# First batch's token mix in the AV banks, beta as masked rows made on chip, and mixing out of the score banks

## The chip, the cores and the metric

The kernel runs on one core of a Trainium2 chip. The metric is the device time of one launch in microseconds (us), as the median of several executions. TensorE (PE) does the matmuls, VectorE (DVE) and ScalarE (ACT) the elementwise work, GpSimd (POOL) casts, copies and issues of converting loads, SyncE (SP) issues of plain loads, stores and DMA transposes.

## The reference

Eight batches of grouped-query attention (16 query heads on 4 key/value heads, 384 positions, head width 64) feed a residual MLP with affine steps over 1024 channels and 4096 hidden channels:

```python
attn = softmax(q @ k.T / sqrt(64)); x = (attn @ v) with heads side by side   # 384 x 1024
a1  = alpha1 * x + beta1
tok = einsum('ts,bsd->btd', w_tok, a1)
u   = x + lam * tok
a2  = alpha2 * u + beta2
out = u + lam * (relu(a2 @ w_ch1) @ w_ch2)
```

## The kernel before

**Stages.** `side(b)` returns a list of small units of work for batch b: transposes of k and q, scores, exp, AV, the token mix and the transposes of a2. `main(b)` is the channel MLP of batch b: 32 h matmul groups (L393, eight matmuls of 128x384 each) and then six output groups (L417, 32 matmuls of 128x512 each). Batch 0's units run alone at the start; batch b+1's units are slipped between the matmuls of `main(b)` at a steady pace. The order of each engine's instructions is the order of the program: `manual_schedule` reorders nothing, and each engine runs its queue in that order.

**Pairs.** Attention works on pairs of heads: `NP` = 8 pairs, each 128 channels. `scores(i)` (L202) fills 1024 score columns and ACT takes their exp (L211). `av_piece(p, hh)` (L236) gives one pair's AV; VectorE divides by the sum (`rinv` L241, `x` L242) and forms a1 (L246 in batch 0, L249 and L251 later). `tok(p)` (L258) mixes the pair over positions; VectorE adds it to x (L265) and forms a2 (L270). `a2_transpose(p)` turns a2 for the h matmuls, either as a DMA transpose issued by SyncE (L274) or on PE with an ACT copy (L280, L283).

**PSUM.** The eight banks are four tags: "sc" has two buffers of two banks (scores, and batch 0's first h groups), "mm" two of one bank (h, output groups, warm-up, and batch 0's AV), "av" and "tp" one bank each. A tile with the tag of another waits until that one has been read. Before the change `tok` takes "av" in batch 0 and "sc" later; `spread` (vectors) takes "tp" or "av".

**Batch 0's vectors.** alpha1*lam, alpha2, beta1*lam and lam are loaded as 24 rows (three copies of eight rows of 128) into `rows_f`, and `split` (L496 to L503) parts each into three bf16 rows that add up to the float32 value. `spread` multiplies them with a selector `sel`, which broadcasts a row over the 128 partitions, and ACT copies the result into `vecs` (L312). beta1 enters batch 0's mix another way: `rows_r` (L298 to L302) makes row sums of the transposed w_tok in two bf16 parts, `R`, and `H` holds beta in rows; one matmul of R by H for each third of the output adds the term (L262). H is filled by three small DMAs at the end of the second `split` (L505).

**Order in batch 0.** The dictionary `at` says which steps follow which `scores(i)`. Three pairs of q are transposed early, `spread` of the lower pairs follows scores 2 and 4, w_tok's transposes (`wtok_transpose`, L289 and L292) follow scores 4 and 5. At the end of `side(0)` the list of `a2_transpose`, `tok(6)`, `tok(7)` and `h_part` (the first four h groups, L147, cut by the eight pairs of channels they read) overlaps the mix of the last pairs with the first h matmuls. Pairs 0 to 3 of a2 go by DMA transpose, pairs 4 to 7 by PE.

**Weights.** w_ch1 comes in 16 chunks a batch through a ring of five buffers, by GpSimd's queue (L126); chunk c+5 is issued once chunk c has been used. w_ch2 is loaded once, in slices between batch 0's chunks (L131), and the next batch's q and v follow in the same queue (L108, L102).

Of the kernel before, what the change touches and what calls it, by code (L numbers as in the profile page):

```python
# [12 lines left out]
def kernel(  # L13
# [21 lines left out]
    nc = tc.nc  # L35
    f32 = mybir.dt.float32
# [11 lines left out]
    P = 128  # L48
# [86 lines left out]

    late = []


    early = {}

# [12 lines left out]
    def side(b):  # L153
# [11 lines left out]

        def bc(t, p):
            return t[:, None, cols(p)].to_broadcast([P, NST, P])

        def evac(eng):
            return nc.scalar.copy if eng == "ACT" else nc.vector.tensor_copy  # L170

        def k_transpose(h0, eng="DVE"):
            k2 = k2s[b]
# [77 lines left out]
            nc.vector.tensor_tensor(out=a1s[p], in0=t, in1=bc(h1, p), op=ADD)  # L251

        def tok(p):
            ps = psum.tile([P, NST, P], f32, tag="av" if first else "sc", name="tok",
                           bufs=1 if first else 2)
            for tt in range(NST):
                for st in range(NST):
                    nc.tensor.matmul(out=ps[:, tt, :], lhsT=wtokT[:, st, tt * P:(tt + 1) * P],  # L258
                                     rhs=a1s[p][:, st, :], start=(st == 0),
                                     stop=(st == NST - 1 and not first))  # L260
                if first:
                    nc.tensor.matmul(out=ps[:, tt, :], lhsT=R[:, tt * P:(tt + 1) * P],  # L262
                                     rhs=H[:, cols(p)], start=False, stop=True)
            u = x[:, :, cols(p)]
            nc.vector.tensor_tensor(out=u, in0=ps, in1=u, op=ADD)  # L265
            if first:
                a2s[p] = hTf[:, 7296 + p % 5 * S:7296 + (p % 5 + 1) * S].rearrange("p (a d) -> p a d", a=NST)
            else:
                a2s[p] = sb.tile([P, NST, P], bf, tag="a2", name="a2", bufs=3)
            nc.vector.tensor_tensor(out=a2s[p], in0=u, in1=bc(al2, p), op=MUL)  # L270

        def a2_transpose(p):
            if not pe_flip or first and p < NP - 4:
                nc.sync.dma_start_transpose(  # L274
                    out=a2T[:, p, :S].rearrange("p (a s) -> p a s", a=NST),
                    in_=a2s[p].rearrange("p a d -> p (a d)"))
                return
            ps = tp_ps([P, NST, P])
            for tt in range(NST):
                nc.tensor.matmul(out=ps[:, tt, :], lhsT=a2s[p][:, tt, :], rhs=ident,  # L280
                                 is_transpose=True, start=(tt == 0), stop=(tt == NST - 1),
                                 skip_group_check=True)
            nc.scalar.copy(out=a2T[:, p, :S], in_=ps.rearrange("p a b -> p (a b)"))  # L283
# [8 lines left out]
            nc.vector.tensor_copy(out=wtokT[:, st, :], in_=ps.rearrange("p a b -> p (a b)"))  # L292


        def rows_r(tag):
            ps = psum.tile([P, S], f32, tag=tag, name="r", bufs=1)
            for st in range(NST):
                nc.tensor.matmul(out=ps[:3], lhsT=ones3, rhs=wtokT[:, st, :], start=(st == 0),  # L298
                                 stop=(st == NST - 1))
            t = hTf[:3, 10240:10240 + S]  # L300
            nc.vector.tensor_copy(out=t, in_=ps[:3])
            nc.vector.scalar_tensor_tensor(out=R[:3], in0=t, scalar=neg3, in1=ps[:3], op0=MUL, op1=ADD)  # L302


        def spread(ps_, vs, tag, eng="ACT"):
# [18 lines left out]
        if not first:  # L324
            if pe_flip:
                add(k_transpose, 0)
                add(q_transpose, 0)
                add(k_transpose, 2)
                add(q_transpose, 2)
                if b == 1:  # L330
                    add(split, 3, 4)
            for j in range(NP + 4):
                if 1 < j < NP + 2:
                    add(av_piece, j - 2, 0)
                    add(av_piece, j - 2, 1)
                if j <= NP:
                    add(scores2, j)
                    if pe_flip and j in (1, 3):
                        add(q_transpose, 4 + 2 * (j // 2))
                if 2 < j < NP + 3:  # L340
                    add(tok if pe_flip else tok_flip, j - 3)
                if pe_flip and j > 3:
                    add(a2_transpose, j - 4)
                if b == 1 and j < 2:
                    for p in (4 * j, 4 * j + 2):
                        add(spread, (p, p + 1), (2, 4), "tp")
                elif j < 2:
                    us.extend([lambda: None] * 2)
            return us
# [1 line left out]
        add(q_transpose, 0, 1, "DVE", "av")  # L351
        add(q_transpose, 1, 1, "DVE", "tp")
        lower, upper = range(NP // 2), range(NP // 2, NP)
        at = {1: [(warmup, 3), (split, 0, 1), (split, 1, 3)], 2: [(warmup, 2), (spread, lower, (0, 1), "tp"), (warmup, 2)],
              3: [(q_transpose, 2, 2, "DVE", "av")],
              4: [(spread, lower, (1, 2), "tp"), (wtok_transpose, 0, "av"), (wtok_transpose, 1, "tp")],
              5: [(wtok_transpose, 2, "av"), (rows_r, "tp")],
              7: [(q_transpose, 4, 2, "ACT")], 8: [(k_transpose, 2, "ACT"), (spread, upper, (0, 1), "av")],
              10: [(q_transpose, 6, 2, "ACT")], 12: [(spread, upper, (1, 2), "tp")]}
        for i in range(18):  # L360
            add(scores, i)
            for f, *a in at.get(i, []):
                add(f, *a)
            for p in range(NP):
                last = (9 * p + 8) // 4
                if i == last + 1:
                    add(av_piece, p, 0)
                    add(av_piece, p, 1)
                if i == last + 4:
                    add(tok_flip if p < NP - 4 else tok, p)  # L370
        add(av_piece, NP - 1, 0)
        add(av_piece, NP - 1, 1)
        for f, *a in ((a2_transpose, 4), (tok, 6), (a2_transpose, 5), (h_part, (0, 1), range(4)), (tok, 7),
                      (a2_transpose, 6), (h_part, (2, 3), range(4)), (h_part, range(4), (4, 5)),
                      (a2_transpose, 7), (h_part, range(4), (6,)), (h_part, range(4), (7,))):
            add(f, *a)
        return us

# [51 lines left out]
    with tc.manual_schedule(engines=order):  # L430
# [9 lines left out]
        load_k(0, [0])  # L440

        hTf = hT.rearrange("p n s -> p (n s)")
        rows_f = hTf[:24, 9216:10240].bitcast(f32)
        rows_t = hTf[:24, 10240:11264].bitcast(f32)
        rows_b = hTf[:, 11264:11776]
        stage = sb.tile([P, NST * DM], f32, tag="x", name="stage", bufs=2)
        qst, vst = (stage[:, i:i + Hkv * NST * D].rearrange("p (h st d) -> p h st d", h=Hkv, st=NST)
# [2 lines left out]
        be2 = stage[:, 2112:2112 + NDT]  # L450
        R = stage[:, 2120:2312].bitcast(bf)
        H = stage[:, 2312:2824].bitcast(bf)
        ones3 = stage[:, 2824:2826].bitcast(bf)[:, :3]
        neg3 = stage[:3, 2826:2827]
        masks = [stage[:24, 2827 + i:2828 + i] for i in range(2)]
        sel = stage[:, 2829:2833].bitcast(bf)
        for t in (stage[:, 2120:2824], rows_b, sel):
            nc.vector.memset(t, 0.0)
        nc.sync.dma_start(out=vst, in_=v[0].rearrange("h (p st) d -> p h st d", st=NST))

        for i, ap in enumerate((moe_alpha1, moe_alpha2, moe_beta1, moe_lam)):
            nc.sync.dma_start(out=rows_f[:, i * P:(i + 1) * P],
                              in_=bass.AP(tensor=ap.tensor, offset=ap.offset, ap=[[0, 3], [P, NP], [1, P]]))
        load_k(0, [2])
        with nc.allow_non_contiguous_dma(reason="one small vector, once"):
            nc.sync.dma_start(out=be2, in_=moe_beta2.rearrange("(dt di) -> di dt", di=P))
# [11 lines left out]

        load_q4(1)
        make_identity(nc, ident)  # L480
        nc.gpsimd.memset(ones3, 1.0)
        nc.gpsimd.tensor_scalar(out=neg3, in0=ident[:3, 1:2], scalar1=-1.0, scalar2=None, op0=MUL)
        for t in vt:
            nc.vector.memset(t[:, :, :, D:], 1.0)
        AX = mybir.AxisListType.X
        for i, m in enumerate(masks):
            nc.vector.tensor_reduce(out=m, in_=ident[:24, 8 * (i + 1):24], op=ADD, axis=AX)
        with nc.allow_low_precision("ones and zeros"):
            nc.vector.tensor_reduce(out=sel[:24], in_=ident[:24, :24].rearrange("p (k c) -> p c k", k=3), op=ADD, axis=AX)

        def split(lo, hi):
            c = slice(lo * P, hi * P)
            for i in (0, 2):
                if lo <= i < hi:
                    r = rows_f[:, i * P:(i + 1) * P]
                    nc.vector.tensor_tensor(out=r, in0=r, in1=rows_f[:, 3 * P:], op=MUL)  # L496
            src, dst = rows_f, rows_t
            for m in masks:
                nc.vector.tensor_copy(out=rows_b[:24, c], in_=src[:, c])
                nc.vector.scalar_tensor_tensor(out=dst[:, c], in0=rows_b[:24, c], scalar=m, in1=src[:, c],  # L500
                                               op0=MUL, op1=mybir.AluOpType.subtract)
                src, dst = dst, src
            nc.vector.tensor_copy(out=rows_b[:24, c], in_=src[:, c])  # L503
            for i, k in enumerate((0, 0, 1)) if lo <= 2 < hi else ():
                nc.sync.dma_start(out=H[i:i + 1], in_=rows_b[8 * k:8 * k + 8, 2 * P:3 * P])  # L505

        place_k(0, 0)
        for h, cp in ((0, nc.vector.tensor_copy), (2, nc.scalar.copy)):
# [81 lines left out]
```

## Time and profile before

| | |
|---|---|
| median of 9 runs | 823.04 us (821.86 to 824.46) |
| profiled execution | 824.29 us |
| its span | 822.2 us, mean granted clock 0.993 |
| batch 0's units alone | first 50 us of the span |
| software DMA queue | 83.28 MB, 87.8% of 16 engines' span |

The page gives busy time by engine, and the span in 40 slices of 20.6 us each. A wait is named by the waiting engine, its tile and line, and what came last. The granted clock is PE's, as a share of full speed. Matmul ends are modelled, so a PE that is shown busy may still wait a little; start-to-start times of groups are safer than their lengths.

### The profile page before, as it was taken

Reading aid. Unit: us, or ns where it says so; the run is one execution under the profiler, and the core shown is the slowest. Engines: PE = TensorE matmul, PEld = TensorE weight load, DVE = VectorE, ACT = ScalarE, POOL = GpSimd, SP = SyncE. Lnnn points to the kernel's source line nnn. Section 1 sums busy time; section 2 is a strip of 40 time slices with the busy share of each in tenths; the row PEclk is TensorE's granted clock in tenths of the full one; section 3 lists DMA queues with packets and bytes.
Section 4 is the critical chain, followed back from the end, with each engine's and each line's share of the span. In section 5 each row is a group of like instructions: output and inputs, shape, how many; then the busy total and the mean of one; then the engine's idle time right before and its main releaser. Section 6 shows DMA issues by size and latency. Waiting matters only on the chain.

```text
span 822.2 us, 14049 instructions
## 1 busy us (share of the span) xinstructions
PE 802.1 (98%) x6072; PEld 448.3 (55%) x6072; DVE 346.4 (42%) x678; ACT 225.7 (27%) x299; POOL 185.3 (23%) x231
## 2 busy tenths in 40 slices
PE   6789999999999999999999999999999999999997
PEld 3655555565555655566545664556545565556543
DVE  6744545244543444434443344524454344442222
ACT  5725321332103421133212331033210442102100
POOL 6224440124002240022401233022500221003000
PEclk9999999999999999999999999999999999999999
DMA  9999999799949993599927999489994999129610
GB/s 165 199 161 200 201 214 177 122 177 171 93 102 160 177 159 59 130 172 174 146 63 137 180 176 109 98 134 178 174 85 98 147 178 127 36 57 192 87 39 38
DMA packets 261017, 112.94 MB, mean 137 GB/s; under 512 B 110204, under 2 KB 254684, under 8 KB 260956
## 3 DMA queue, kind: packets, MB, share of 16 engines
q0 software_dynamic: 197760, 83.28, 87.8%
q1 hardware_dynamic: 62652, 28.38, 14.2%
q8 instruction: 47, 0.77, 0.4%
q10 hardware_dynamic: 544, 0.39, 0.2%
q14 instruction: 14, 0.11, 0.0%
HBM read 170.51 MB, written 12.58 MB: 223 GB/s over the span
## 4 chain that ended last, share of the span: by engine, by line
PE 88%; DVE 2%; issue 0%; ACT 0%; ACTq 0%; DVEq 0%
PE ch L417 41%; PE h L393 36%; PE av L236 4%; PE sc L202 3%; PE tok L258 3%; DVE a1f L249 1%; DVE x L242 1%; DVE a L251 1%; DVE hT L403 0%; ACT es L211 0%; DVE rinv L241 0%; PE tp L280 0%; DVE o L422 0%; DVE o L423 0%; PE tp L186 0%
## 5 line engine op out<-in xcount | busy, mean ns | idle before, releaser
L417 PE MATMUL ch<-w,hT 128*128 128x512 bf16 x1536 | 353.5, 379 | 0.0
L393 PE MATMUL h<-a2T,w 128*128 128x384 bf16 (+1 forms) x2016 | 349.3, 326 | 0.6
L393 PEld LDWEIGHTS <-w 128*128 128x128 bf16 x2016 | 189.5, 98 | 124.8 <-issue 8.4
L126 POOL DMA_DIRECT2D w<-in_moe_w_ch_dram x128 | 112.6, 880 | 549.4 <-PE h L393 493.5
L417 PEld LDWEIGHTS <-hT 128*128 128x128 bf16 x1536 | 142.5, 98 | 155.2 <-issue 4.6
L211 ACT ACTIVATE es<-sc 128x1024 bf16<-128x1024 f32 x126 | 123.3, 1021 | 281.6 <-PE sc L202 281.6
L403 DVE TENSOR_SCALAR hT<-h,bias 128x384 bf16<-128x384 f32 x128 | 79.0, 617 | 187.1 <-PE h L393 186.5
L401 ACT ACTIVATE hT<-h,bias 128x384 bf16<-128x384 f32 x128 | 74.3, 581 | 227.2 <-PE h L393 202.4
L422 DVE TENSOR_TENSOR o<-ch,vecs 128x512 f32<-128x512 f32 x48 | 33.0, 688 | 92.6 <-PE ch L417 92.5
L265 DVE TENSOR_TENSOR x<-tok,x 128x384 f32<-128x384 f32 x64 | 35.5, 555 | 85.7 <-PE tok L258 77.1
L236 PEld LDWEIGHTS <-es 128*128 128x128 bf16 x1008 | 45.9, 97 | 21.4 <-ACT es L211 0.9
L236 PE MATMUL av<-v,es 128*128 128x65 bf16 x1008 | 49.2, 193 | 0.8 <-ACT es L211 0.8
L258 PEld LDWEIGHTS <-wtokT 128*128 128x128 bf16 x576 | 38.5, 99 | 15.6 <-issue 4.2
L202 PE MATMUL sc<-qT,kT 64*128 64x384 bf16 (+2 forms) x576 | 45.9, 275 | 0.3 <-ACT hT L211 0.3
L241 DVE RECIPROCAL rinv<-av 128x6 f32<-128x6 f32 x64 | 12.3, 192 | 67.6 <-PE av L236 67.3
L258 PE MATMUL tok<-a,wtokT 128*128 128x128 bf16 x504 | 37.3, 219 | 0.9 <-ACT es L211 0.9
L242 DVE TENSOR_TENSOR x<-av,rinv 128x384 f32<-128x384 f32 x64 | 35.6, 557 | 2.3
L202 PEld LDWEIGHTS <-kT 64*128 64x128 bf16 x576 | 20.0, 94 | 27.8 <-issue 23.3
L423 DVE TENSOR_TENSOR o<-o,x 128x512 f32<-128x512 f32 x48 | 33.3, 693 | 1.6
L270 DVE TENSOR_TENSOR a<-x,vecs 128x384 bf16<-128x384 f32 x56 | 31.5, 562 | 1.9
L251 DVE TENSOR_TENSOR a<-a1f,vecs 128x384 bf16<-128x384 f32 x56 | 31.2, 557 | 2.2
L249 DVE TENSOR_TENSOR a1f<-x,vecs 128x384 f32<-128x384 f32 x56 | 31.2, 557 | 1.9
(68 smaller groups left out, 211.6 us busy)
## 6 DMA issues: line engine op xcount, KB each, us to landing
w<-in_moe_w_ch_dram POOLq DMA_DIRECT2D x135, 512.0 KB, 6.5
out_dram<-o SPq DMA_DIRECT2D x48, 256.0 KB, 2.1
q_raw<-in_q_dram POOLq DMA_DIRECT2D x21, 256.0 KB, 7.8
kst<-in_k_dram SPq DMA_DIRECT2D x16, 192.0 KB, 3.0
w<-in_moe_w_ch_dram POOLq DMA_DIRECT2D x10, 256.0 KB, 11.8
w<-in_moe_w_ch_dram POOLq DMA_DIRECT2D x1, 2048.0 KB, 26.4
v<-in_v_dram POOLq DMA_DIRECT2D x21, 64.0 KB, 7.4
a2T<-a SPq DMA_TRANSPOSE x48, 4.5
```

Source lines behind the costliest of these rows:

```text
L126: nc.gpsimd.dma_start(out=t, in_=w1src[:, :, c * CW * P:(c + 1) * CW * P])
L202: nc.tensor.matmul(out=sc[:, hh, k % 4:k % 4 + n], lhsT=kT[r, sk, 2 * p // G, :], rhs=qT[r, st:st + n, p, :], start=True, stop=True)
L211: nc.scalar.activation(out=e, in_=sc, func=EXP, scale=scale_qk)
L236: nc.tensor.matmul(out=av[:, hh, sq, :], lhsT=ess[k // 4][:, hh, k % 4, :], rhs=vb[:, sk, hk, :], start=(sk == 0), stop=(sk == NST - 1))
L242: nc.vector.tensor_tensor(out=x[:, :, cols(p)].rearrange("p st (h d) -> p h st d", h=2), in0=av[:, :, :, :D], in1=rinv.to_broadcast([P, 2, ...
L249: nc.vector.tensor_tensor(out=t, in0=x[:, :, cols(p)], in1=bc(g1, p), op=MUL)
L251: nc.vector.tensor_tensor(out=a1s[p], in0=t, in1=bc(h1, p), op=ADD)
L258: nc.tensor.matmul(out=ps[:, tt, :], lhsT=wtokT[:, st, tt * P:(tt + 1) * P], rhs=a1s[p][:, st, :], start=(st == 0), stop=(st == NST - 1 an ...
L393: nc.tensor.matmul(out=ps[:, :n], lhsT=w1[:, dt, j * P:(j + 1) * P], rhs=a2T[:, dt, :n], start=(dt == 0), stop=(dt == NDT - 1))
L401: nc.scalar.activation(out=hT[:, nt, :], in_=ps[:, :S], func=RELU, bias=c1)
L403: nc.vector.tensor_scalar(out=hT[:, nt, :], in0=ps[:, :S], scalar1=c1, scalar2=0.0, op0=ADD, op1=mybir.AluOpType.max)
L417: nc.tensor.matmul(out=ps, lhsT=hT[:, nt, ms * P:(ms + 1) * P], rhs=w2[:, nt, cs], start=(nt == 0), stop=(nt == NNT - 1))
```

## The change

- In batch 0 `tok` takes "mm", the two banks of the AV, instead of "av". In batch 1 it takes "av", from batch 2 on "tp"; before it took "sc".
- beta's rows `H` are made on VectorE: the parameter loads have four copies of eight rows (32 rows), and eight multiplications of the 32 rows by a column of `sel4` write H (L507 of the changed kernel). The three DMAs go. `rows_r` makes 32 equal rows in place of three, with a mask `masks[2]` for the second part.
- Pair 3 of a2 is transposed by PE as well, odd pairs in "av"; the list at the end of `side(0)` is reordered for it, and `h_part` reads three pairs first instead of four.
- In batch 0's order, the second q transpose goes ahead of the second `split` and of the first `spread`, two warm-up matmuls fall away, and the w_tok transposes alternate banks. In batch 1 the first two q transposes take "av".

```diff
         def tok(p):
-            ps = psum.tile([P, NST, P], f32, tag="av" if first else "sc", name="tok",
-                           bufs=1 if first else 2)
+            tag, n = ("mm", 2) if first else ("av", 1) if pe_flip else ("tp", 1)
+            ps = psum.tile([P, NST, P], f32, tag=tag, name="tok", bufs=n)
...
         def a2_transpose(p):
-            if not pe_flip or first and p < NP - 4:
+            if not pe_flip or first and p < NP - 5:
...
-            ps = tp_ps([P, NST, P])
+            ps = tp_ps([P, NST, P], "av" if first and p % 2 else "tp")
...
         def rows_r(tag):
-                nc.tensor.matmul(out=ps[:3], lhsT=ones3, rhs=wtokT[:, st, :], start=(st == 0),
+                nc.tensor.matmul(out=ps[:32], lhsT=ones, rhs=wtokT[:, st, :], start=(st == 0),
...
-            nc.vector.scalar_tensor_tensor(out=R[:3], in0=t, scalar=neg3, in1=ps[:3], op0=MUL, op1=ADD)
+            nc.vector.scalar_tensor_tensor(out=R[:32], in0=t, scalar=masks[2], in1=ps[:32], op0=MUL, op1=ADD)
...
                 add(k_transpose, 0)
-                add(q_transpose, 0)
+                add(q_transpose, 0, 2, "DVE", "av")
                 add(k_transpose, 2)
-                add(q_transpose, 2)
+                add(q_transpose, 2, 2, "DVE", "av")
...
-        at = {1: [(warmup, 3), (split, 0, 1), (split, 1, 3)], 2: [(warmup, 2), (spread, lower, (0, 1), "tp"), (warmup, 2)],
-              3: [(q_transpose, 2, 2, "DVE", "av")],
-              4: [(spread, lower, (1, 2), "tp"), (wtok_transpose, 0, "av"), (wtok_transpose, 1, "tp")],
-              5: [(wtok_transpose, 2, "av"), (rows_r, "tp")],
+        at = {1: [(warmup, 3), (split, 0, 1)], 2: [(warmup, 2)],
+              3: [(q_transpose, 2, 2, "DVE", "av"), (spread, lower, (0, 1), "tp"), (split, 1, 3)],
+              4: [(wtok_transpose, 0, "av"), (spread, lower, (1, 2), "tp")],
+              5: [(wtok_transpose, 1, "av"), (wtok_transpose, 2, "tp"), (rows_r, "av")],
               7: [(q_transpose, 4, 2, "ACT")], 8: [(k_transpose, 2, "ACT"), (spread, upper, (0, 1), "av")],
-              10: [(q_transpose, 6, 2, "ACT")], 12: [(spread, upper, (1, 2), "tp")]}
+              10: [(q_transpose, 6, 2, "ACT")], 12: [(spread, upper, (1, 2), "av")]}
...
-                    add(tok_flip if p < NP - 4 else tok, p)
+                    add(tok_flip if p < NP - 5 else tok, p)
...
-        for f, *a in ((a2_transpose, 4), (tok, 6), (a2_transpose, 5), (h_part, (0, 1), range(4)), (tok, 7),
-                      (a2_transpose, 6), (h_part, (2, 3), range(4)), (h_part, range(4), (4, 5)),
-                      (a2_transpose, 7), (h_part, range(4), (6,)), (h_part, range(4), (7,))):
+        for f, *a in ((a2_transpose, 3), (tok, 6), (a2_transpose, 4), (h_part, (0, 1), range(3)), (tok, 7),
+                      (a2_transpose, 5), (h_part, (2, 3), range(3)), (h_part, range(4), (3, 4)), (a2_transpose, 6),
+                      (h_part, range(4), (5,)), (a2_transpose, 7), (h_part, range(4), (6,)), (h_part, range(4), (7,))):
...
-                              in_=bass.AP(tensor=ap.tensor, offset=ap.offset, ap=[[0, 3], [P, NP], [1, P]]))
+                              in_=bass.AP(tensor=ap.tensor, offset=ap.offset, ap=[[0, 4], [P, NP], [1, P]]))
...
-            for i, k in enumerate((0, 0, 1)) if lo <= 2 < hi else ():
-                nc.sync.dma_start(out=H[i:i + 1], in_=rows_b[8 * k:8 * k + 8, 2 * P:3 * P])
+            for p in range(NP if lo <= 2 < hi else 0):
+                nc.vector.tensor_scalar(out=H[:32, p * P:(p + 1) * P], in0=rows_b[:32, 2 * P:3 * P],
+                                        scalar1=sel4[:, p:p + 1], scalar2=None, op0=MUL)
```

More of the change, by code (lines that the diff above doesn't have):

```diff
@@ L136, with evac @@
     late = []
+    def evac(eng):
+        return nc.scalar.copy if eng == "ACT" else nc.vector.tensor_copy
     early = {}
@@ L167, in bc @@
             return t[:, None, cols(p)].to_broadcast([P, NST, P])
-        def evac(eng):
-            return nc.scalar.copy if eng == "ACT" else nc.vector.tensor_copy
         def k_transpose(h0, eng="DVE"):
@@ L297, in rows_r @@
             for st in range(NST):
-                nc.tensor.matmul(out=ps[:3], lhsT=ones3, rhs=wtokT[:, st, :], start=(st == 0),
+                nc.tensor.matmul(out=ps[:32], lhsT=ones, rhs=wtokT[:, st, :], start=(st == 0),
                                  stop=(st == NST - 1))
-            t = hTf[:3, 10240:10240 + S]
-            nc.vector.tensor_copy(out=t, in_=ps[:3])
-            nc.vector.scalar_tensor_tensor(out=R[:3], in0=t, scalar=neg3, in1=ps[:3], op0=MUL, op1=ADD)
+            t = hTf[:32, 10240:10240 + S]
+            nc.vector.tensor_copy(out=t, in_=ps[:32])
+            nc.vector.scalar_tensor_tensor(out=R[:32], in0=t, scalar=masks[2], in1=ps[:32], op0=MUL, op1=ADD)
         def spread(ps_, vs, tag, eng="ACT"):
@@ L442 @@
         hTf = hT.rearrange("p n s -> p (n s)")
-        rows_f = hTf[:24, 9216:10240].bitcast(f32)
-        rows_t = hTf[:24, 10240:11264].bitcast(f32)
+        rows_f = hTf[:32, 9216:10240].bitcast(f32)
+        rows_t = hTf[:32, 10240:11264].bitcast(f32)
         rows_b = hTf[:, 11264:11776]
@@ L452 @@
         H = stage[:, 2312:2824].bitcast(bf)
[L453 to L456, printed above, removed]
+        ones = stage[:, 2824:2840].bitcast(bf)
+        masks = [stage[:32, 2840 + i:2841 + i] for i in range(3)]
+        sel4 = stage[:32, 2844:2852]
+        sel = stage[:, 2852:2856].bitcast(bf)
         for t in (stage[:, 2120:2824], rows_b, sel):
@@ L480 @@
         make_identity(nc, ident)
-        nc.gpsimd.memset(ones3, 1.0)
-        nc.gpsimd.tensor_scalar(out=neg3, in0=ident[:3, 1:2], scalar1=-1.0, scalar2=None, op0=MUL)
+        nc.gpsimd.memset(ones, 1.0)
         for t in vt:
@@ L486 @@
         for i, m in enumerate(masks):
-            nc.vector.tensor_reduce(out=m, in_=ident[:24, 8 * (i + 1):24], op=ADD, axis=AX)
+            nc.vector.tensor_reduce(out=m, in_=ident[:32, 8 * (i + 1):24 + 8 * (i // 2)], op=ADD, axis=AX)
+        nc.vector.tensor_scalar(out=masks[2], in0=masks[2], scalar1=-1.0, scalar2=None, op0=MUL)
         with nc.allow_low_precision("ones and zeros"):
-            nc.vector.tensor_reduce(out=sel[:24], in_=ident[:24, :24].rearrange("p (k c) -> p c k", k=3), op=ADD, axis=AX)
+            for t, n in ((sel, 24), (sel4, 32)):
+                nc.vector.tensor_reduce(out=t[:n], in_=ident[:n, :n].rearrange("p (k c) -> p c k", c=NP), op=ADD, axis=AX)
         def split(lo, hi):
@@ L497, in split @@
             src, dst = rows_f, rows_t
-            for m in masks:
-                nc.vector.tensor_copy(out=rows_b[:24, c], in_=src[:, c])
-                nc.vector.scalar_tensor_tensor(out=dst[:, c], in0=rows_b[:24, c], scalar=m, in1=src[:, c],
+            for m in masks[:2]:
+                nc.vector.tensor_copy(out=rows_b[:32, c], in_=src[:, c])
+                nc.vector.scalar_tensor_tensor(out=dst[:, c], in0=rows_b[:32, c], scalar=m, in1=src[:, c],
                                                op0=MUL, op1=mybir.AluOpType.subtract)
                 src, dst = dst, src
-            nc.vector.tensor_copy(out=rows_b[:24, c], in_=src[:, c])
-            for i, k in enumerate((0, 0, 1)) if lo <= 2 < hi else ():
-                nc.sync.dma_start(out=H[i:i + 1], in_=rows_b[8 * k:8 * k + 8, 2 * P:3 * P])
+            nc.vector.tensor_copy(out=rows_b[:32, c], in_=src[:, c])
+            for p in range(NP if lo <= 2 < hi else 0):
+                nc.vector.tensor_scalar(out=H[:32, p * P:(p + 1) * P], in0=rows_b[:32, 2 * P:3 * P],
+                                        scalar1=sel4[:, p:p + 1], scalar2=None, op0=MUL)
         place_k(0, 0)
```

## The prediction

> **What bounds the kernel now.** I read the page first, then the waits of the TensorE, then the windows of its clock, then the timelines of the opening.
>
> ```profile
> PE 802.1 (98%) x6072; PEld 448.3 (55%) x6072; DVE 346.4 (42%) x678; ACT 225.7 (27%) x299; POOL 185.3 (23%) x231
> ...
> PE   6789999999999999999999999999999999999997
> ```
>
> TensorE (PE) is busy all the way from slice 4 on. The only loose slices are the first three, 0 to 60 us, which hold batch 0's attention and mixing. In 250 to 350 us it is busy 99.90 of 100 us. So later batches can give almost nothing, and each microsecond has to come from the opening or from the few named waits. PE's waits in 20 to 60 us, then in 60 to 160 us (us, times, longest):
>
> ```profile
> PE h L147 <- DMA a2T<-hT: 2.6, 1, 2.6
> PE tok L258 <- ACT vecs L312: 1.4, 1, 1.4
> ...
> PE tok L262 <- DMA stage<-hT: 1.1, 1, 1.1
> PE tp L186 <- DVE kT L179: 0.6, 1, 0.6
> ```
>
> ```profile
> PE tok L258 <- ACT es L211: 0.9, 1, 0.9
> PE av L236 <- ACT es L211: 0.8, 1, 0.8
> ```
>
> All but the last are waits that the change touches. The clock makes them dearer. Windows of its clock (length, then PE busy; the third number from the end is the granted clock):
>
> ```profile
> 8.25:11.66 3.41, 1.54 (x14) 0.72 (x15) 3.14 (x9) 2.27 (x4) 3.41 (x5) 1.00 0.99 130
> 11.66:15.07 3.41, 3.41 (x39) 2.52 (x40) 2.65 (x8) 1.90 (x3) 3.41 (x6) 0.50 1.21 134
> ...
> 18.48:21.90 3.42, 2.32 (x44) 1.71 (x40) 2.78 (x6) 1.75 (x2) 0.00 (x0) 1.00 1.32 228
> 21.90:25.31 3.41, 1.47 (x25) 1.11 (x22) 1.42 (x4) 3.09 (x5) 0.00 (x0) 1.00 1.44 201
> 25.31:28.72 3.41, 3.41 (x41) 2.31 (x38) 1.85 (x4) 1.19 (x2) 0.00 (x0) 0.50 1.41 191
> 38.96:42.38 3.42, 1.07 (x13) 0.71 (x11) 2.32 (x6) 0.68 (x2) 0.00 (x0) 1.00 1.43 195
> 42.38:45.79 3.41, 3.13 (x20) 2.27 (x20) 0.04 (x1) 0.00 (x0) 0.00 (x0) 0.50 2.37 159
> ```
>
> A stretch of 3.41 us with PE busy 1.54 us or less is followed by one at clock 0.50; 2.32 us busy is not. A stall long enough is paid twice.
>
> **The change, part by part.** The sum is made against the profiled execution, 824.29 us (span 822.2, 2.1 around it). That run is 1.25 above the median of nine, 823.04.
>
> *A. The opening to the last AV (ends 38.3).* Beta's rows. The three small DMAs (2.28 us of SyncE issue) go, and with them PE's 1.1 us wait, which ended at 20.08. In their place eight masks (32x128) stand on VectorE, behind the second split and ahead of pair 0's AV. VectorE's timeline has these nearest rows:
>
> ```profile
> 8.71 0.54 DVE L499 CAST hT<-hT 24x128 bf16<-24x128 f32 x1
> 9.29 0.34 DVE L500 SCALAR_TENSOR_TENSOR hT<-hT,stage 24x128 f32<-24x128 bf16 x1
> ```
>
> The same cast takes 0.20 at 58.89, where GpSimd is idle. The smallest reduces take 0.115. A mask costs 0.115 to 0.54; I take 0.20, the row of the same size without GpSimd. In order from the first split's end at 10.88: qT copy 0.57, second split 2.3, masks 1.6, rinv, x and a1 1.45, first wtokT copy 0.4, then one transpose and two copies 1.2, row sums 0.35, two R steps 1.2: R at 19.95, against 20.08. The new wait is for R, behind VectorE, in place of the DMA: gain 0.1 (from -2.6 at 0.54 to +0.8 at 0.115). But PE now idles before wtokT (about 14.3 to 17.2), so the following window probably drops to 0.50: up to 1.7, taken 1.5.
>
> Mixing leaves the "av" bank, so tok(1) no longer waits for the vector copy (1.39). Scores(9) behind it need kT, copied by ACT until 24.51, so they start at 24.55 and not 26.21: 1.65. The dropped window 25.31 to 28.72 goes too, but ACT then binds: two exps 2.1, qT 0.82, two exps 2.1, vecs 0.65, five exps 5.32 from 24.6 end at 35.6 in place of 37.76. Gain 2.1. A = 0.1 + 2.1 - 1.5 = 0.7; ends -2.2 and 2.9.
>
> Hidden: two more reduces and a multiply on VectorE before 4.04 (0.4, under its 1.0 us wait for the k load; uncovered, 0.4). The parameter loads have 32 rows for 24: SyncE issues them in 0.70 to 0.86 each, so 0 to 0.25 more each; I take 0, since the k load issues far more rows in 0.45; uncovered, up to 1.0 on the masks and on the second k load behind them. The row sums have 32 rows for 3 but the same length: 0.
>
> [...]
>
> *B. The first h matmuls.* Pair 3's transpose moves from SyncE (issued 32.6, waited for until 42.66, 10.1 later) to PE. The wait of 2.62 goes. So does the low window behind it: 2.95 us of work ran at 0.50, so 1.45. PE gets three matmuls, 0.17; ACT one copy of 0.48, in its idle 5.95 before 46.01. Late next is pair 2's transpose: issued at 30.92 less A, 30.2, it lands 8.8 (that pair was not waited for before) to 10.1 later, 39.0 to 40.3; its first reader is due at 39.2. Wait 0 to 1.1, taken 0.3. B = 2.62 + 1.45 - 0.17 - 0.3 = 3.6; ends 0 and 4.0. Batch 0's main loop starts 0.7 + 3.6 = 4.3 earlier, at 45.7.
>
> *C. Batch 1's transposes.* q goes to "av" and no longer waits for the k copy: from 51.62 to 53.69 eight h matmuls needed 2.07 where 1.31 is usual: 0.77. It cannot go before q has landed (48.7; 48.2 with one transpose fewer in the queues); it is due at 48.6. Lead 5.1.
>
> *D. Mixing of batch 1.* tok(1) waits for a score bank until 92.51: eight h matmuls and the wait took 2.39 for 1.30: 1.09. In "av" its bank is read empty at 89.6. Lead 6.1. Two lesser such waits (108.4, 125.2) give 0.33. The new sharing costs: tok(0) is read by 85.98, the next AV comes at 86.31, 0.3 to spare; tok(6) at 132.62 meets its AV's reading until 132.75: 0.2. Net 0.1. The 0.8 us wait of the AV stays.
>
> *E. The weight stream caps the lead.* From 52 us on, the software queue is full (about 0.20 MB per us). The last of batch 0's weight chunks:
>
> ```profile
> w<-in_moe_w_ch_dram POOLq DMA_DIRECT2D x1, 512.0 KB, 12.8
> ```
>
> It is issued at 81.38, lands at 94.2, is used at 96.06: spare 1.86. With PE earlier the stream starts earlier only where the queue stood idle: from its q and v loads' end (49.3, less 0.5 for the transpose) to its real start, 52.6 (0.26 MB by 54): 3.8. So PE can lead by 1.86 + 3.8 = 5.7, not 6.1.
>
> *F. Batches 2 to 7.* Mixing takes the "tp" bank, idle there. No PE wait names the score banks; the largest irregularity is 0.17 per batch, before an h bank. 0, between -1.0 and +1.0 (six batches).
>
> Sum: 5.7 + 0.1 = **5.8**, so 824.29 - 5.8 = **818.5**. The cap makes the sum insensitive: B a microsecond less moves it by 0.6. Its outer end, without cap: 2.9 + 4.0 + 0.77 + 1.09 + 0.1 = 8.9, 815.4, a little less where a run starts from the median.
>
> **The rivals.**
> - *Another wait at the same h matmuls.* Pair 2's transpose, or pair 7's last step on VectorE, keeps PE idle as long as pair 3's did, with the clock drop. Then B is -0.17 and the lead 0.7 - 0.17 + 0.77 + 1.09 + 0.1 = 2.5: 821.8. For: landings stretch (7.5 to 10.1) as the queues fill. Against: pair 2 was not waited for.
> - *The weights decide.* If the stream starts no earlier, all of it is hidden behind 1.86: 2.0 in all, 822.3. For: the queue is full on both sides. Against: it shows 8% in 50 to 52.
> - *Slower: VectorE becomes the opening's bound.* Place: the masks between the second split and pair 0's AV; queued behind them are rinv, x, a1, the wtokT copies and R, and PE waits for all. At m us a mask, A is 0.7 - s with s = 8(m - 0.2). Pair 2's transpose then lands at 30.92 - A + 10.1 = 41.0 - A and the low window stays; 30 h matmuls 4.9, one mixing 0.65, three transposes 0.5 and the clock 1.45 put the main loop at 48.5 - A, a lead of 1.5 + A over 49.97. With C, D and the rest the gain is 4.2 - s: gone at m = 0.72, clearly slower (1.65) from 0.93. With each mask held by a GpSimd copy (0.86) besides its own 0.20, m = 1.06: 2.7 slower, 827.0. For: 0.20 becomes 0.54 beside GpSimd. Against: GpSimd has only some 2.5 us of copies left there.
>
> **How the numbers follow.** The forecast 0.72; another wait 0.11, weights 0.09, VectorE 0.08. About 0.2% (1.65 us) is what a measurement of this kernel can tell from no change. Faster: the forecast, half of the first rival and a third of the second, 0.81; same 0.11; slower 0.08. The range reaches from 815.2 (outer sum) to 822.3 (the second rival), leaving out the slower case and the tails.
>
> **What would show it.** Right: no wait of h on a transpose DMA, or under 1.1 us; no PE wait of tok on ACT; main loop's first h near 45.7; R near 20; masks near 0.20 each; one low clock window, near 18 to 22, in place of three; around 96 us a short PE wait on weights. Wrong: masks over 0.5, a wait over 2 us in 37 to 43, the first w chunk of the main loop landing no earlier than 57, or any new PE wait after 150 us.

## The result, and the profile after

The changed kernel takes 819.72 us (median of 9 runs, 818.69 to 821.64); the kernel before takes 823.97 us (29 runs, 821.26 to 825.23). The ratio is 0.9951, 95% interval 0.9941 to 0.9962: about 4.0 us less. Measured once more, beside before, it gave 820.34 against 822.99, ratio 0.9959 [0.9943, 0.9974].

The profiled execution of after took 818.27 us (span 816.4), 6.0 less than the profiled 824.29 of before. So the two profiles differ by more than the medians do (4.25 and 2.65); why is the last thing that the experiments show.

The page of after, PE's row and its slices:

```profile
PE 798.6 (98%) x6073; PEld 446.2 (55%) x6073; DVE 351.1 (43%) x689; ACT 226.1 (28%) x300; POOL 184.8 (23%) x230
...
PE   5999999999999999999999999999999999999997
```

The loose part is now the first slice alone; slices 2 and 3, at 7 and 8 tenths before, are full. PE's waits of after, first in 0 to 60 us, then in 60 to 822 us (us, times, longest):

```profile
PE tp L289 <- DVE wtokT L292: 4.2, 1, 4.2
PE vec L311 <- DVE hT L505: 1.7, 2, 1.2
...
PE h L394 <- ACT hT L402: 0.4, 1, 0.4
```

```profile
PE av L236 <- ACT es L211: 0.8, 1, 0.8
```

No h matmul waits for a DMA transpose, no mix for a vector copy or a score bank. What stands in their place is the 4.2 us before w_tok's transposes, and VectorE's timeline (start, us) says what VectorE did meanwhile, with GpSimd's copies beside it:

```profile
13.12 0.33 DVE L505 CAST hT<-hT 32x256 bf16<-32x256 f32 x1
13.48 3.33 DVE L507 TENSOR_SCALAR stage<-hT,stage 32x128 bf16<-32x128 bf16 x8
```

```profile
13.29 0.88 POOL L478 COPY q_raw<-qh 128x768 bf16<-128x768 bf16 x1
14.08 0.99 POOL L98 CAST k<-kst 128x384 bf16<-128x384 f32 x2
15.00 0.83 POOL L478 COPY q_raw<-qh 128x768 bf16<-128x768 bf16 x1
15.77 0.21 POOL L523 CAST a2T<-stage 128x8 bf16<-128x8 f32 x1
15.90 0.89 POOL L126 DMA_DIRECT2D w<-in_moe_w_ch_dram  x1
```

Eight masks take 3.33 us, 0.42 each in the mean and not 0.20. One by one they are very unequal: the first four end at 14.22, 14.66, 15.11 and 15.88, each 0.05 after the end of a GpSimd copy (14.17, 14.61, 15.06, 15.83), and the last two at 16.79 and 16.82, when GpSimd's issue of a load ends (16.79); the two between take 0.24 and 0.23. `rinv`, `x`, a1 and the first wtokT copy queue behind them, and PE waits for that copy. R ends at 21.68 (forecast 19.95; the beta DMAs of before were waited for until 20.08). The clock pays too, in windows of 3.41 us (length, PE busy; the third number from the end is the granted clock):

```profile
11.55:14.97 3.42, 1.51 (x22) 0.80 (x18) 3.24 (x8) 2.32 (x4) 3.42 (x6) 1.00 1.45 177
14.97:18.38 3.41, 0.00 (x0) 0.00 (x0) 3.23 (x10) 0.48 (x1) 2.96 (x5) 0.50 1.43 187
18.38:21.80 3.42, 3.26 (x31) 2.02 (x30) 1.94 (x5) 0.00 (x0) 0.00 (x0) 0.50 1.35 207
```

Two windows at half clock in a row, where one was forecast; before had three, at 11.7, 25.3 and 42.4.

Where the time came from, by the start of the same instruction in both traces:

| place | before | after | lead |
|---|---|---|---|
| scores(9) | 26.21 | 26.60 | -0.39 |
| end of batch 0's AVs | 38.32 | 37.85 | 0.47 |
| main loop's first h | 49.97 | 45.41 | 4.56 |
| h after batch 1's q transposes | 54.02 | 49.28 | 4.74 |
| batch 1, tok(1) | 92.51 | 86.99 | 5.52 |
| first output group | 99.59 | 94.08 | 5.51 |
| batch 1, tok(5) | 126.22 | 120.41 | 5.81 |
| batch 1, tok(6) | 132.62 | 126.99 | 5.63 |
| end of the span | 822.2 | 816.4 | 5.8 |

### The profile page after: what moved, and what is told of

It is laid out like the page before. It is cut to its first block, busy times and chain, and to the rows that moved or that the text cites. A ratio compares the mean times of both kernels' runs of the same rounds, so it can differ in the third digit from the quotient of the medians.

```text
span 816.4 us, 14047 instructions
## 1 busy us (share of the span) xinstructions
PE 798.6 (98%) x6073; PEld 446.2 (55%) x6073; DVE 351.1 (43%) x689; ACT 226.1 (28%) x300; POOL 184.8 (23%) x230
## 4 chain that ended last, share of the span: by engine, by line
PE 89%; DVE 2%; issue 0%; ACT 0%; ACTq 0%; DVEq 0%
PE ch L418 41%; PE h L394 37%; PE av L236 4%; PE sc L202 4%; PE tok L258 3%; DVE x L242 0%; DVE a1f L249 0%; DVE a L251 0%; DVE hT L404 0%; PE tp L280 0%; DVE rinv L241 0%; ACT es L211 0%; DVE o L423 0%; DVE o L424 0%; PE tp L186 0%
```

## The experiments

**Theory.** The gain is two waits removed, pair 3's transpose and the tok banks, less an opening that VectorE makes late. The masks are slow because GpSimd copies beside them. Batch 1's Q, or the weight stream, limits what a still earlier opening brings. **Rivals:** a mask of 32 partitions simply costs 0.42; the low clock windows, not VectorE, hold PE back; one part alone does it all.

### The parts one by one

*The tail alone* (e1_tail) on the kernel before:

```diff
-            if not pe_flip or first and p < NP - 4:
+            if not pe_flip or first and p < NP - 5:
```

and the reordered list at the end of `side(0)`, as in the change.

> The kernel before with the tail alone: pair 3 of a2 on PE and the reordered list, nothing else. If the wait of the h matmuls on pair 3's DMA transpose (2.62 us) and the low clock window behind it (1.45) were lost time, the main loop starts 3.0 to 3.9 us earlier (0.17 for the extra transpose, 0 to 1.1 for pair 2's landing), and the kernel is 3.0 to 3.9 us faster than before. Rival, another wait takes the place (pair 2's transpose or VectorE's last steps): under 1 us faster, with a PE wait of over 1.5 us between 38 and 43 us.

Measured: 820.84 against 822.63, ratio 0.9976 [0.9961, 0.9991], about 2.0 less. The wait on the transpose is gone. Less than expected, and the profiled execution, at 824.55, lies above all the others of this kernel (819.54 to 821.41): the beta DMAs took 3.1 us of waiting in it instead of 1.1, and its mean granted clock was 0.990, where the nine others have 0.994 to 0.998.

*The later batches alone* (e2_later) on the kernel before (tok in "av" and "tp", batch 1's q in "av"):

```diff
-            ps = psum.tile([P, NST, P], f32, tag="av" if first else "sc", name="tok",
-                           bufs=1 if first else 2)
+            tag, n = ("av", 1) if pe_flip else ("tp", 1)
+            ps = psum.tile([P, NST, P], f32, tag=tag, name="tok", bufs=n)
```

> The kernel before with the later batches' banks alone: batch 1's mixing and its first two q transposes in av, mixing from batch 2 on in tp. By the sum of C and D, 0.77 + 1.09 + 0.1 = 2.0 us faster, all of it before 130 us and nothing from 150 us on. Weights spare 1.86 us at the last chunk, so they would just allow it. Rival, the waits only move to the exp or to the av bank: under 0.5 us, with a new PE wait of av or tok between 60 and 135 us.

Measured: 821.40, ratio 0.9985 [0.9969, 1.0002], about 1.2 less, with an interval that just reaches no change. In 60 to 160 us only the AV's 0.8 us wait is left, as in after; in 20 to 60 us two waits of the opening stand as they did, and the one for the beta DMA is 0.4 instead of 1.1:

```profile
PE h L147 <- DMA a2T<-hT: 2.5, 1, 2.5
PE tok L258 <- ACT vecs L312: 1.4, 1, 1.4
```

*Batch 0's mix back in one bank* (e4_tok_av): after, with `tok` in "av", a2's transposes and the last `spread` in "tp".

```diff
-            tag, n = ("mm", 2) if first else ("av", 1) if pe_flip else ("tp", 1)
+            tag, n = ("av", 1) if pe_flip else ("tp", 1)
```

> The changed kernel with batch 0's mixing back in the av bank (the second upper spread and all a2 transposes back in tp). If the bank is what batch 0's mixing waited for, the wait of tok(1) on the vector copy (about 1.4 us) is back with a low window after it, and the kernel is 1.5 to 2.5 us slower than the changed one. Rival, ScalarE sets the pace there anyway: under 0.5 us slower.

Measured: 821.62, ratio 0.9983 [0.9969, 0.9997]. Set against after's 0.9951 and 0.9959, the AV's banks are worth about 2.0 to 2.6 us (each ratio's difference by 823, with over 1 us of uncertainty in it). The removed wait is back:

```profile
PE tok L258 <- ACT vecs L313: 1.4, 1, 1.4
```

This execution also shows the masks with and without GpSimd beside them, for its first copy had to wait for a load:

```profile
13.54 3.24 DVE L507 TENSOR_SCALAR stage<-hT,stage 32x128 bf16<-32x128 bf16 x8
14.20 0.86 POOL L478 COPY q_raw<-qh 128x768 bf16<-128x768 bf16 x1 [0.81 <-DMA qh<-in_q_dram]
```

The first four masks, before 14.20, start 0.16 us apart; the fifth, started at 14.19, ends at 15.10, 0.04 after that copy, and the other three end with the copies behind it.

So the parts come to some 2.0 (tail), 1.2 (later batches), 2.0 to 2.6 (AV's banks): 5.2 to 5.8. The whole gives 3.4 to 4.0 by its two ratios. The difference, if it is more than the intervals and if the parts add up, is what the rest of the opening, the masks and their order, costs; no run shows that they add up.

### What the masks cost

*Beta's rows by three DMAs again* (e3_dma_rows), 32 rows otherwise:

```diff
-            for p in range(NP if lo <= 2 < hi else 0):
-                nc.vector.tensor_scalar(out=H[:32, p * P:(p + 1) * P], in0=rows_b[:32, 2 * P:3 * P],
-                                        scalar1=sel4[:, p:p + 1], scalar2=None, op0=MUL)
+            for i, k in ((0, 0), (1, 1), (24, 0)) if lo <= 2 < hi else ():
+                nc.sync.dma_start(out=H[i:i + 1], in_=rows_b[8 * k:8 * k + 8, 2 * P:3 * P])
```

> The changed kernel with beta's rows brought by three small DMAs again, as before the change, in place of the eight masks on VectorE. If the masks (3.33 us on VectorE) are what delays the w_tok copies and so PE's 4.2 us idle, that idle falls to about 1 us, mixing of pair 0 starts at about 20.7 (13.5 + the 7.2 that the DMAs took before, issue to release) in place of 21.95, and at most one window near 15 to 22 us has the low clock; the main loop leads by 1 to 1.5 us more. If the weight stream caps the lead at 5.7 us at the last chunk, only 0.2 to 0.5 us of this reaches the end and PE waits for weights near 88 to 93 us; if there is no cap, the kernel is 1 to 1.5 us faster than the changed one. Rival, the masks cost nothing that counts: the same opening within 0.3 us.

Measured: 819.51, ratio 0.9963 [0.9947, 0.9978]. The wait before w_tok's transposes falls from 4.2 to 1.1 us, the mix waits 1.4 us for the DMA, and the main loop starts at 43.97, 1.44 ahead of after. The span is only 0.5 shorter (815.9); a new wait takes 1.0:

```profile
PE tp L186 <- DMA q_raw<-in_q_dram: 1.0, 1, 1.0
```

*The masks behind the row sums* (e5_mask_late): same instructions, `mask_rows` after `rows_r`.

```diff
-              5: [(wtok_transpose, 1, "av"), (wtok_transpose, 2, "tp"), (rows_r, "av")],
+              5: [(wtok_transpose, 1, "av"), (wtok_transpose, 2, "tp"), (rows_r, "av"), (mask_rows,)],
```

> The changed kernel with its eight masks moved behind the row sums' second step, where GpSimd has no copy left (its last issue ends at 17.9). If the masks took 0.42 each because GpSimd was at work beside them, they take 0.12 to 0.20 here, PE's idle before the w_tok transposes falls from 4.2 to about 1 us, mixing of pair 0 starts near 20.4 and the kernel is 0.3 to 1 us faster than the changed one. Rival, 0.42 is the operation's own time: the masks end near 22.1, mixing starts no earlier than in the changed kernel, and the time is the same within 0.5 us.

Measured: 818.47, ratio 0.9945 [0.9931, 0.9960], span 815.7. VectorE's timeline, where GpSimd no longer copies:

```profile
18.82 1.37 DVE L509 TENSOR_SCALAR stage<-hT,stage 32x128 bf16<-32x128 bf16 x8
```

0.17 each. The same eight instructions cost 0.42 beside GpSimd and 0.17 alone: the rival that 0.42 is the instruction's own falls, here and in e4_tok_av. The main loop starts at 43.57; the q transposes then wait 1.6 us for Q, until 48.36.

*The masks as one instruction* (e6_mask_one; a tensor_tensor of 32x1024, operands broadcast):

```diff
-                nc.vector.tensor_scalar(out=H[:32, p * P:(p + 1) * P], in0=rows_b[:32, 2 * P:3 * P], ...
+                nc.vector.tensor_tensor(out=H[:32].rearrange("p (n d) -> p n d", n=NP),
+                                        in0=rows_b[:32, None, 2 * P:3 * P].to_broadcast([32, NP, P]),
+                                        in1=sel4[:, :, None].to_broadcast([32, NP, P]), op=MUL)
```

> The changed kernel with the eight masks as one broadcast multiplication of 32x1024. By the rows of VectorE (128x384 in 0.56) it takes about 1.2 us where the eight took 3.33; R is about 2 us earlier (near 19.6), PE's idle before w_tok about 2 us, main loop about 1 to 1.5 us earlier. If q's landing caps batch 1's first transposes (lead 5.5 there, as the run with the DMA rows showed), the total gains only 0.4 to 0.9 us over the changed kernel; without a cap 1 to 2 us. Rival: an instruction of 1024 elements beside GpSimd is held as long as the eight were, no gain.

Measured: 819.00, ratio 0.9952 [0.9936, 0.9967], span 818.0. The instruction takes 1.21 us, yet the main loop starts at 47.01, where 43.9 to 44.4 was expected. VectorE's timeline of this kernel shows another victim:

```profile
13.26 2.86 DVE L505 CAST hT<-hT 32x256 bf16<-32x256 f32 x1
```

The last cast of the split, 0.33 in after, lasts 2.86 here and ends at 16.12.

*The same with w_tok's copies on ACT* (e7_one_act):

```diff
-            nc.vector.tensor_copy(out=wtokT[:, st, :], in_=ps.rearrange("p a b -> p (a b)"))
+            nc.scalar.copy(out=wtokT[:, st, :], in_=ps.rearrange("p a b -> p (a b)"))
```

> The one-instruction mask and the three w_tok copies on ScalarE, idle there from 15.4 to 22.1. PE no longer waits for VectorE between the w_tok transposes; R near 17.5, mixing of pair 0 near 17.6 in place of 21.95, main loop at 42 to 43 in place of 45.4. If q's landing is the cap, PE waits for it 2 us or more at batch 1's first q transpose and the total is 0.5 to 1 us better than the changed kernel, no more than the one-instruction mask alone. If there is no cap: 2.5 to 3.5 us better.

Measured: 818.60, ratio 0.9942 [0.9922, 0.9962], span 816.9. Again a cast of the split is held, 2.85 from 13.05, and PE waits 4.6 us for the vectors; the main loop starts at 46.30, where 42 to 43 was expected.

By their times none of these four kernels is told apart from after: their ratios, 0.9942 to 0.9963, stand beside after's 0.9951 and 0.9959, and all the intervals overlap. So the runs show what an instruction costs beside GpSimd, but not what the masks cost the kernel.

### What an earlier opening can bring

*Batch 0's side work later* (e9_lead), on top of the last kernel:

```diff
-            lead, span = (0.04, 0.82) if b == 0 else (0, 0.95)
+            lead, span = (0.07, 0.79) if b == 0 else (0, 0.95)
```

> As the run before, but batch 1's units begin about 3 us later in batch 0's main loop (lead 0.07 in place of 0.04), so that q has landed. The wait on q is gone. If the weight stream is the next cap (lead 5.7 to 6.5 at the last chunk), PE waits for weights between 80 and 95 us and the total stays within 0.5 us of the run before. If weights were never near, the early main loop counts in full and it is 1.5 to 2.5 us faster than the run before.

Measured: 818.70, ratio 0.9949 [0.9930, 0.9967]. A cast is held here too (2.64), the main loop starts at 45.44, and h groups that now follow one another directly wait 1.1 us for ACT to empty a bank. No wait on weights near 93 us, and no gain over the run before: neither branch of the expectation came.

*Masks behind the row sums, side work later* (e10_late_lead):

> The kernel after with the masks behind the row sums (as in e5_mask_late), and batch 0's side work started at 7% of the main loop instead of 4%. Theory (the lead of an earlier opening stops at the landing of batch 1's Q, near 48.2 us): the 1.6 us wait of the q transposes on Q's transfer is gone, at the price of up to 1 us of an h matmul waiting for the copies of the transposes; the lead at batch 1's first tok is 6.3 to 7.3 us over before instead of about 5.5, and the span 0.5 to 1.5 below e5's 815.7. Rival (the cap of 5.7 us by the expert weights, from the prediction): the channel matmuls near 93 us wait for weights and the span stays within 0.3 of 815.7.

Measured: 818.34 against 822.99, ratio 0.9939 [0.9923, 0.9954], span 816.3. The theory's number is missed and the rival's mechanism is missed too. The wait for Q is gone, the 1.1 us wait for ACT has come for it, and a cast is held 2.85 us, so the main loop starts at 45.74. The lead at batch 1's first mix is 3.0 (81.50 against 84.50) and not 6.3 to 7.3, for its own work begins later; at the first output group it is 6.0, and nothing waits for weights.

*Masks behind the row sums, 16 matmuls more to hold the clock* (e11_late_warm):

```diff
             ps = psum.tile([P, 4, P], f32, tag=tag, name="vec", bufs=1)
+            for _ in range(8 if vs == (1, 2) and ps_[0] == 0 else 0):
+                nc.tensor.matmul(out=ps[:, :2], lhsT=ident, rhs=kT[:, 0, 0:2, :], start=True, stop=True)
```

and eight more ahead of scores(5), in its tile.

> e5_mask_late with 16 matmuls more of 128x256 (about 0.11 us each at full clock, 1.7 in all), written into tiles that are overwritten at once, where TensorE waits between 12 and 16 us. Theory (two windows of half clock, 6.8 us from 15, cost 2 to 3 us of matmuls because the window before them held too little work): the granted clock stays at 1.00 from 11 to 22 us, the main loop starts 1.5 to 3 us ahead of e5's 43.57, the wait for Q's landing grows by as much from its 1.6 us, and the end is within 0.4 of e5's span of 815.7. Rival (the opening's matmuls wait for DVE and ACT and not for the clock): the main loop starts within 0.5 of 43.57, or later.

Measured: 819.38, ratio 0.9959 [0.9945, 0.9973], span 816.9. A cast is held 2.85 us. Two low windows became one (15.35 to 18.77), but the window before still had only 1.25 us of PE work in it, and the filler of scores(5) ran in the low one. From the start of the held cast to the main loop it is 32.14 us, against 32.41 in e10_late_lead, which has the same hold: a low window less, net of the filler, is worth 0.3 there. The main loop starts at 45.23, behind e5_mask_late's 43.57 because of the hold; the expected 1.5 to 3 us are not found. The q transposes wait 1.1 us for Q, until 49.55. What a low window costs without any filler stays open.

*Both* (e12_late_warm_lead):

> e11_late_warm with batch 0's side work started at 7% of the main loop. Theory (Q's landing alone holds back the lead): the wait for Q is under 1 us, the lead over before at batch 1's first tok is 7 to 9 us, the channel matmuls near 92 us do not wait for weights, and the span is 1.5 to 3 below e5's 815.7: 813 to 814.5. Rival (weights): a wait of the channel matmuls for a weight transfer takes all beyond a lead of 5.7 to 6.3, and the span is 815 to 816.

Measured: 818.38, ratio 0.9940 [0.9924, 0.9956], span 816.0. Lead at the first output group 6.3, no wait on weights, cast held 2.85. The wait of 1.1 us between h groups is there as in e9_lead and e10_late_lead. The theory's numbers are missed: the lead at batch 1's first mix is 3.3 (81.17) and not 7 to 9, the span 816.0 and not 813 to 814.5. The rival's span (815 to 816) is met, but not by a wait for weights.

### The kernel after once more

> The kernel after once more, unchanged, beside before. Theory (the executions differ by where the 3.41 us windows of the TensorE clock fall, and the profile shown of before had three low windows where most executions have one or two): median 819.0 to 820.5, ratio to before 0.994 to 0.9975, profiled span 815.5 to 819 with a clock of .993 to .998 that goes with it. Rival (the profiles stand for the medians): 817.5 to 818.5, ratio 0.992 to 0.994.

Measured: 820.34 (six runs: 818.45, 819.52, 820.22, 820.46, 820.51, 820.53), ratio 0.9959 [0.9943, 0.9974]. The medians differ less than the first profiles, as the theory had it, but the clock is the same in both profiles of this kernel (.996) while this execution, 820.22, is 1.95 longer. VectorE's timeline shows what is different:

```profile
13.19 2.86 DVE L501 CAST hT<-hT 32x256 bf16<-32x256 f32 x1
16.09 0.47 DVE L502 SCALAR_TENSOR_TENSOR hT<-hT,stage 32x256 f32<-32x256 bf16 x1
16.59 0.42 DVE L505 CAST hT<-hT 32x256 bf16<-32x256 f32 x1
17.05 1.75 DVE L507 TENSOR_SCALAR stage<-hT,stage 32x128 bf16<-32x128 bf16 x8
```

GpSimd's copies, in the same execution:

```profile
13.36 0.88 POOL L478 COPY q_raw<-qh 128x768 bf16<-128x768 bf16 x1
...
15.81 0.32 POOL L523 CAST a2T<-stage 128x8 bf16<-128x8 f32 x1
```

A cast that starts at 13.19 ends at 16.05, with GpSimd's run of copies and not after the first of them. Once they are over the eight masks take 1.75, 0.16 from start to start but for one pause of 0.53, which ends with GpSimd's issue of a load (16.92 to 18.08). R ends at 23.74 (21.68 in the first profile), the main loop starts at 47.35 (45.41), the span is 818.3 (816.4). Held casts show in 7 of the 11 profiles of kernels with the 32-row opening, and in none of the three with the opening of before, whose last cast starts at 12.59 to 12.65 and ends before the copies begin (13.4 to 13.7). The new order puts that cast, or in e0_again and e7_one_act the one two instructions before it, at 13.05 to 13.4; in e4_tok_av it ends before the copies begin (14.20). Held or not held is not fixed by the kernel: it starts 0.17 us ahead of the first copy in e5_mask_late (0.33 long) as in e10_late_lead (2.85).

## Why the prediction was right, and where not

The direction and the range held, and the forecast of 818.5 is 1.2 below the median. Of the steps:

**A, the opening: the mis-sized term.** The step took 0.20 for a mask, "the row of the same size without GpSimd", in a stretch where GpSimd was copying. It measured 0.42 (3.33 in all against 1.6), R came at 21.68 instead of 19.95, and two windows were low instead of one. The removed bank wait was sized about rightly (2.1; the reverse experiment gives 2.0 to 2.6). So A was 0.47 in the first profile, not 0.7, and in the second, with the cast held, about 1.5 below zero (0.47 less the 1.94 that separates the two main loops). The row at 58.89 that gave 0.20 was not free of GpSimd, which issued a load from 58.34 to 59.04; the next cast of that size, at 59.50, takes 0.21 with nothing beside it, so the price holds. That step also missed that the neighbours could be hit: it put the second split at its old length, and an instruction of 0.33 became 2.86.

**The masks beside GpSimd.** That they wait for it is shown, by the ends of the first four in after, each 0.05 behind the end of a copy, and by the four of e4_tok_av that ran before its first copy, 0.16 apart; what in the chip makes them wait no run shows. With a copy of 0.86 for each mask besides its own 0.20 the third rival came to 1.06, an estimate from the timelines of before; the mean was 0.42, between that and the 0.20 that I chose. R came 1.7 and 3.8 later than forecast in the two profiles of after, and the gains by the two ratios are 4.0 and 3.4. A held cast of 2.86 us outlasts every single copy (0.99 for two, 0.88 for one); why a cast is held for the whole run of copies stays open.

**B, the tail: 4.1 (forecast 3.6).** The lead grew from 0.47 to 4.56. Pair 2's transpose cost no wait; 0.3 had been set aside. Alone, the tail gave 2.0 by its ratio. Part of the term was the low window behind the stall, 1.45, and that is not in every execution: in e2_later, whose batch 0 is that of before, the same 2.5 us wait fell across two windows, and neither the one it began in nor the next dropped the clock:

```profile
36.65:40.06 3.41, 1.74 (x28) 1.38 (x25) 2.96 (x7) 0.96 (x2) 0.00 (x0) 1.00 1.26 192
40.06:43.47 3.41, 2.54 (x26) 1.88 (x26) 0.83 (x2) 0.48 (x1) 0.00 (x0) 1.00 1.88 178
43.47:46.88 3.41, 3.41 (x24) 2.04 (x23) 1.44 (x5) 0.91 (x3) 0.00 (x0) 1.00 2.44 156
```

The main loop of that execution starts at 46.74, 3.23 ahead of the profile of before, with nothing changed in batch 0. So up to that much of the 4.56 which the profiles credit to A and B can be the executions' own, and the sizes of A and B are no firmer than that; that the waits are gone, and that they cost time, rests on the profiles of after and on the ratios of e1_tail and e4_tok_av.

**C, batch 1's transposes: a limit of the right kind, the gain smaller.** The wait for the k copy went as forecast (eight h matmuls take 1.31 again where they took 2.07), but 0.6 of it came back at once: from the q transposes to the next h it is 0.92 instead of 0.33, with the 0.4 us wait for ACT's copy to hT. The limit was put at a landing of 48.2, a lead of about 5.5. Openings that were early enough ran into it: the transposes wait until 48.24 and 48.36 in the two profiles that start the main loop before 44, and the lead behind them is 5.6 and 5.4. After itself, at 4.74, does not get there. Nor is the landing the same in all executions: in e11_late_warm the transposes wait until 49.55.

**D, mixing of batch 1: right.** From 60.61 to tok(1) the lead grew from 4.45 to 5.52, 1.07 for a forecast 1.09; tok(6) cost 0.18 for 0.2.

**E, the cap by the weights: too tight.** It was put at 5.7. After never reached it, so it took nothing from the sum; leads of 6.0 to 6.3 at the first output group, in five other kernels, show no wait for weights, and the short wait near 96 us that was to be its sign did not come.

**F, batches 2 to 7: right,** no change and no new wait.

That the profile agrees with the sum (5.8 of span, forecast 5.8) is in part luck: A (0.2 below) and C to E (1.0 instead of 1.4) are made up by B (0.5 above) and by what follows batch 1's first mixes (0.3 instead of 0.1). The medians agree less, since after's first profile was faster than all nine timed runs (818.27, median 819.72) and before's slower than its median (824.29, median 823.97 and, in the runs shown at first, 823.04). By the medians the gain is 3.4 to 4.0, 1.8 to 2.4 less than the sum: within the range, but below the forecast.

## What to carry to other kernels

Price an instruction by the row that has the same neighbours on the other engines, not by the shortest row of its size; and when a chain is moved or lengthened by half a microsecond, look what it now runs beside. A stage can be a microsecond late without the kernel showing it where the next limit, here Q's landing, does not come earlier with it: with the main loop's start at 43.57 or at 45.41, 1.84 apart (e5_mask_late and after), the ends were 0.7 apart. Before a difference between two profiles is taken for a gain, a second profile of the same kernel shows how much of it is the execution's own.

## What the runs showed of the hardware

- Casts of 32x256 on VectorE, 0.33 to 0.79 us in these profiles otherwise, were held 2.64 to 2.86 us in 7 of the 10 profiles in which one met a run of GpSimd copies. Small products by a scalar (the masks) started 0.16 apart without GpSimd (the first four of e4_tok_av), and beside it ended one by one, 0.04 to 0.05 after each of its copies (after and e4_tok_av). A 128x384 product with an operand in PSUM took 0.56 beside them (before, at 14.17), and 0.56 without them (at 19.17).
- The low stretches of the clock lasted 3.41 us each in before (the first 11.66 to 15.07) and twice that in after (14.97 to 21.80), and where they begin differs from execution to execution: they start at 11.66, 25.31 and 42.38 in before, four and five times 3.41 apart, and only one, at 16.18, shows in e2_later, whose opening is the same (mean granted clock 0.998, against 0.993).
- How much work keeps the clock up cannot be read from PE's busy time alone: a full-speed window with 1.69 us of it (e5_mask_late, 11.65 to 15.06) was followed by one at 0.50 and one with 1.74 (e2_later, above) was not, but in e2_later the window from 12.77 to 16.18, with 2.10, was followed by one at 0.50 too.
